# Top-k attention with an ELU feed-forward block: a prologue in written order on two queues, five smaller decoding buffers, and decoding moved to later steps

## The chip, the cores and the metric

The kernel runs on one core of a Trainium2 chip. The metric is the device time of one execution in microseconds (us). The engines are TensorE (PE, with its weight loads shown as PEld), VectorE (DVE), ScalarE (ACT), GpSimd (POOL) and SyncE (SP). SP here only issues DMAs.

## What is computed

Eight batches of eight heads, 576 rows, head size 64. For each row of scores only those at or above the 32nd largest enter the softmax. The result, put together to 4608 tokens of 512 values, goes through a feed-forward block with ELU between two matrix products. The weights `w_in` (512 x 2048) and `w_out` (2048 x 512) arrive as 64-bit floats.

```python
scores = scale * np.matmul(q, k.transpose(0, 1, 3, 2))
kth = np.partition(scores, -top_k, axis=-1)[..., -top_k:-top_k + 1]
scores = np.where(scores >= kth, scores, -1000000000.0)
attn = np.exp(scores - np.max(scores, axis=-1, keepdims=True))
attn = attn / (np.sum(attn, axis=-1, keepdims=True) + 1e-09)
x = np.matmul(attn, v)            # then (B,H,S,D) -> (B*S, H*D)
h = x @ w_in
g = np.where(h > 0.0, h, np.exp(np.minimum(h, 0.0)) - 1.0)
out = g @ w_out
```

## The kernel before

**Steps.** The attention work is cut into steps, each one tile of up to 128 query rows for two heads (a head pair). The scores of a step are 2 x 128 x 576. In step n the program makes the scores of step n + 2 (`scores`: eight PE products on L300, two ACT copies on L308), finds the 32 largest of each row of step n on DVE, and finishes steps n - 1 and n - 2: mask and exponential on ACT (`mask`, L369 and L370, after two small POOL operations, L366 and L368), division on POOL (`normalise`, L380 to L387), transposes (`turn`, L406 and L407), the product with v (`attend`, L432). Finding the 32 largest of a row takes four rounds of MAX8 with three MATCH_REPLACE8 between them (`select_row`: L319, L323, L329; `select`: L341, L346, L353).

**Two stages.** The first eight steps (`tight = 8`) cover two query tiles of batch 0: steps 0 to 3 are query tile 0 for the four head pairs, steps 4 to 7 query tile 1. They use `select_row`, and the order of instructions on each engine is left to a scheduler that works from priorities. From step 8 on `manual_schedule` keeps the order as written on PE, ACT, DVE and POOL.

**Feed-forward pieces.** When all heads of a block of tokens are through, `finish` (which copies the attention result to an `xT` tile) puts its feed-forward pieces on a list. `hidden` is one 128-wide slice of the hidden layer: PE products L490, three ACT operations (L502 to L504) that write `n` and `gT`, and later one DVE operation, the gate (L471), which closes it. `project` is a quarter of the second product (L513). `feed`, called four times a step, takes pieces from the list by their costs and due times, once the weights they need are marked as decoded. At most four `n` tiles are unclosed at once.

**Decoding.** The weights are 32 pieces of 128 x 512 64-bit floats. `load_weight` brings one into a `raw` tile by one DMA of 512 KB (L152). `convert_first` takes the exponent part to `e` and the low word to the mantissa part `m` by three ACT operations (L169, L170, L171) and a clamp on POOL (L172). `convert_last` shifts `e` (L179) and joins it with the high word (L182) on DVE, and POOL adds `e` and `m` into the weight tile (L186). `decode_piece(i)` loads piece i + 2, converts the first half of piece i and the last half of piece i - 1. `hook`, called from the selection, runs one `decode_piece`: after rounds 0 and 2 of each row, so four in a step. 33 calls end in step 8, where the memory of the raw tiles goes to the feed-forward pools `f`, `g` and `x`.

A raw tile is `4 * WN` words per partition, with three buffers: two parts for the 64-bit words, one for `e`, one for `m`.

```python
words = t[:, 0 : 2 * WN].rearrange("p (n w) -> p n w", w=2)
return words[:, :, 0], words[:, :, 1], t[:, 2 * WN : 3 * WN], t[:, 3 * WN :]
```

**Prologue.** All loads go to SP's queue in this order: k and q of head pair 0, weight pieces 0 and 1, k and q of pair 1, v of pair 0, then the rest. Each k or q of a head pair is three DMAs (128, 128 and 32 KB). `transpose_qk` turns k and q of a pair by PE (L258, L270) and copies them by ACT (L263, L276); then come the scores of step 0, and the same for pair 1 and step 1. This part too is left to the scheduler.

Of the kernel before, what the change touches and what calls it, by code (L numbers as in the profile page):

```python
# [8 lines left out]
AF = mybir.ActivationFunctionType  # L9
# [71 lines left out]
def kernel(  # L81
# [36 lines left out]
    small = pool("small", 4)  # L118
    xtpool = pool("xt", 2)
    opool = pool("o", 1)  # L120
# [7 lines left out]
    earlyf = raws.enter_context(tc.tile_pool(name="earlyf", bufs=4))  # L128
    rawpool = raws.enter_context(tc.tile_pool(name="raw", bufs=3))

# [19 lines left out]
    def load_weight(i):  # L150
        t = rawpool.tile([P, 4 * WN], U32, tag="raw", name="raw")
        nc.sync.dma_start(t[:, 0 : 2 * WN], weight(i)[0])  # L152
        raw[i] = t

    def parts(t):
        words = t[:, 0 : 2 * WN].rearrange("p (n w) -> p n w", w=2)
        return words[:, :, 0], words[:, :, 1], t[:, 2 * WN : 3 * WN], t[:, 3 * WN :]

    def convert_first(i):

        lo, hi, e, m = parts(raw[i])
# [4 lines left out]
        nc.gpsimd.tensor_scalar(  # L172
            ef, ef, (2.0 - 2.0**-3 - 2.0**-23) * 2.0**-32, 2.0**-63, ALU.min, ALU.max
        )

    def convert_last(i):
        t, dst = raw.pop(i), weight(i)[1]
        lo, hi, e, m = parts(t)
        nc.vector.tensor_scalar(  # L179
            e, e, 0x0FFFFFFF, 3, ALU.bitwise_and, ALU.logical_shift_left  # L180
        )
# [33 lines left out]
    def load_qk(b, hp):  # L215

        for name, src in (("k", k), ("q", q)):
            n = J + 1 if name == "k" else J
            t = ldpool.tile([P, n, 2, D], FP32, tag=name + "in", name=name + "in")
            if name == "k":  # L220
                last = t
            for hh in range(2):
                nc.sync.dma_start(
                    t[:, 0:J, hh, :],
                    src[b, 2 * hp + hh, 0:JP, :].rearrange("(p j) d -> p j d", j=J),
                )
            nc.sync.dma_start(
                last[0:R, J, :, :] if name == "k" else last[R:P, J, :, :],
                src[b, 2 * hp : 2 * hp + 2, JP:S, :].rearrange("h p d -> p h d"),
            )  # L230
            loaded[b, hp, name] = t
# [81 lines left out]
    def select_row(u, i):  # L313
# [8 lines left out]
        for r in range(TOP_K // 8 - 1):  # L322
# [130 lines left out]
    def finish(blk, parts, at, cols, src):  # L453
        if blk.xT is None:
            if blk.slots == 1 and late:
                blk.xT = late["x"].tile([P, NC, P], FP32, tag="xT", name="xT")
            else:
                blk.xT = xtpool.tile([P, NC, T], FP32, tag="xT", name="xT")
# [181 lines left out]
    for n in range(NS + 3):  # L640
# [22 lines left out]
        if n == tight:  # L663
            E = mybir.EngineType
            ctx.enter_context(
                tc.manual_schedule(engines={E.PE, E.Activation, E.DVE, E.Pool})
            )
        passes = select(cur) if cur else iter(range(4))
# [61 lines left out]
```

## Time and profile before

| | us |
|---|---|
| median of 3 runs | 1694.66 |
| range of the 3 runs | 1693.64 to 1695.99 |
| the profiled execution, its time | 1695.23 |
| the profiled execution, its span | 1693.4 |

Over the span PE is busy 1597.5 us (94%), DVE 1542.7 (91%), ACT 1179.6 (70%) and POOL 627.0 (37%). The span is the time from the first to the last instruction in the trace; the execution's own time has 1.83 us more around it. A group of instructions is given by its line in the program, its engine, its operation and the tiles it writes and reads. A row of a table by stretches gives, for each stretch of time, how long each engine was busy in it and with how many instructions (in brackets), then the clock that was granted to PE as a share of full speed, the busy share of the DMA engines and what they moved in GB/s. A line of the chain of waits names a piece of work that the end of the run depended on, with its start and its length.

Some rows that are used later, from the groups of the decoding lines (lowest, median and highest duration in ns over all 32 pieces):

| line | engine | operation | ns |
|---|---|---|---|
| L169 | ACT | absolute value of the high word | 647 / 673 / 706 |
| L170 | ACT | low word to float | 643 / 666 / 727 |
| L171 | ACT | float to integer | 612 / 620 / 661 |
| L172 | POOL | clamp | 612 / 612 / 1142 |
| L179 | DVE | mask and shift | 400 / 426 / 1487 |
| L182 | DVE | join with the high word | 667 / 677 / 1227 |
| L186 | POOL | add, to `w_in` | 1258 / 1270 / 1320 |

One operation begins before the one ahead of it on its engine has fully ended, so the distance from start to start on ACT and DVE is some 0.08 to 0.11 us shorter than the duration.

### The profile page before, as it was taken

Reading aid. Unit: us, or ns where it says so; the run is one execution under the profiler, and the core shown is the slowest. Engines: PE = TensorE matmul, PEld = TensorE weight load, DVE = VectorE, ACT = ScalarE, POOL = GpSimd, SP = SyncE. Lnnn points to the kernel's source line nnn. Section 1 sums busy time; section 2 is a strip of 40 time slices with the busy share of each in tenths; the row PEclk is TensorE's granted clock in tenths of the full one; section 3 lists DMA queues with packets and bytes.
Section 4 is the critical chain, followed back from the end, with each engine's and each line's share of the span. In section 5 each row is a group of like instructions: output and inputs, shape, how many; then the busy total and the mean of one; then the engine's idle time right before and its main releaser. Section 6 shows DMA issues by size and latency. Waiting matters only on the chain.

```text
span 1693.4 us, 26805 instructions
## 1 busy us (share of the span) xinstructions
PE 1597.5 (94%) x8560; PEld 1035.0 (61%) x8560; DVE 1542.7 (91%) x3248; ACT 1179.6 (70%) x2813; POOL 627.0 (37%) x1719
## 2 busy tenths in 40 slices
PE   4568899999999999999999999999999999999999
PEld 3355676667575666756557575755557575755565
DVE  6889999999999999999999999999998999998600
ACT  5787776778776776857758585867758686857531
POOL 3675333343333333433333333333333333332200
PEclk8568999999999999999999999999999999999999
DMA  5531021001200111001100111001100000000000
GB/s 156 169 130 63 15 56 36 7 1 42 51 12 7 29 35 42 1 14 42 43 19 1 28 42 35 7 10 46 36 20 8 21 21 28 7 7 7 7 13 13
DMA packets 101131, 56.25 MB, mean 33 GB/s; under 512 B 84096, under 2 KB 92288, under 8 KB 100992
## 3 DMA queue, kind: packets, MB, share of 16 engines
q1 hardware_dynamic: 100992, 54.55, 11.7%
q8 instruction: 68, 1.11, 0.3%
q14 instruction: 71, 0.58, 0.1%
HBM read 45.09 MB, written 9.44 MB: 32 GB/s over the span
## 4 chain that ended last, share of the span: by engine, by line
PE 68%; DVE 21%; ACT 5%; issue 2%; POOL 2%; DMA 1%; SPq 0%; ACTq 0%; POOLq 0%; DVEq 0%
PE ops L513 25%; PE hps L490 21%; PE avps L432 8%; DVE wk L346 7%; PE scps L300 7%; DVE m L353 6%; PE eps L406 5%; DVE m L341 2%; DVE gT L471 1%; DVE wk L323 1%; DVE m L329 1%; PE qkps L270 1%; ACT sc L370 1%; ACT sc L369 1%; ACT et L407 1%
## 5 line engine op out<-in xcount | busy, mean ns | idle before, releaser
L353 DVE MAX8 m<-wk 128x8 f32<-128x576 f32 x816 | 574.9, 745 | 0.0
L490 PE MATMUL hps<-xT,w_in 128*128 128x256 f32 (+2 forms) x2432 | 554.3, 376 | 19.3 <-ACT gT L503 19.3
L513 PE MATMUL ops<-w_out,gT 128*128 128x512 f32 x1152 | 522.6, 598 | 0.0
L490 PEld LDWEIGHTS hps<-xT,w_in 128*128 128x128 f32 x2432 | 409.5, 194 | 119.9 <-ACT gT L503 26.4
L346 DVE MATCH_REPLACE8 wk<-m,wk 128x576 f32<-128x576 f32 x544 | 399.4, 741 | 0.0
L513 PEld LDWEIGHTS ops<-w_out,gT 128*128 128x128 f32 x1152 | 208.4, 190 | 232.8 <-issue 201.0
L380 POOL TENSOR_SCALAR dene<-den 128x2 f32<-128x2 f32 x144 | 34.9, 243 | 819.6 <-ACT sc L370 819.0
L369 ACT ACTIVATE sc<-sc,neg 128x576 f32<-128x576 f32 x288 | 226.5, 787 | 56.6 <-POOL neg L366 56.1
L370 ACT ACTIVATE sc<-sc,gap 128x576 f32<-128x576 f32 x288 | 223.2, 775 | 26.6 <-ACT sc L369 1.9
L308 ACT ACTIVATE sc<-scps 128x576 f32<-128x576 f32 x288 | 173.4, 661 | 82.4 <-PE scps L300 82.4
L387 POOL TENSOR_SCALAR sc<-sc,rec 128x576 f32<-128x576 f32 x288 | 218.7, 769 | 15.2 <-POOL rec L385 0.4
L300 PE MATMUL scps<-kqT 64*128 64x288 f32 (+1 forms) x1280 | 198.1, 438 | 21.5 <-ACT sc L308 14.7
L471 DVE SCALAR_TENSOR_TENSOR gT<-n,gT 128x256 f32<-128x256 f32 (+2 forms) x304 | 129.1, 431 | 95.3 <-ACT n L504 95.3
L407 ACT COPY et<-eps 128x512 f32<-128x512 f32 x288 | 167.4, 581 | 61.8 <-PE eps L406 61.8
L406 PEld LDWEIGHTS eps<-ident,sc 128*128 128x128 f32 x1152 | 144.5, 145 | 93.4 <-issue 48.9
L346 DVE MATCH_REPLACE8 wk<-m,sc 128x576 f32<-128x576 f32 x272 | 199.7, 741 | 0.0
L432 PE MATMUL avps<-et,vT 128*64 128x256 f32 (+2 forms) x2080 | 191.0, 325 | 9.0 <-ACT et L407 8.4
L406 PE MATMUL eps<-ident,sc 128*128 128x128 f32 x1152 | 177.9, 280 | 21.8 <-POOL sc L387 18.6
L341 DVE MAX8 m<-sc 128x8 f32<-128x576 f32 x272 | 191.3, 744 | 0.0
L432 PEld LDWEIGHTS avps<-et,vT 128*64 128x64 f32 x2080 | 122.3, 140 | 80.4 <-issue 24.7
L502 ACT ACTIVATE n<-hps 128x256 f32<-128x256 f32 (+2 forms) x304 | 112.6, 370 | 84.2 <-PE hps L490 79.0
L300 PEld LDWEIGHTS scps<-kqT 64*128 64x128 f32 (+1 forms) x1280 | 106.0, 180 | 90.2 <-issue 45.1
(47 smaller groups left out, 1236.6 us busy)
## 6 DMA issues: line engine op xcount, KB each, us to landing
kin<-in_k_dram SPq DMA_DIRECT2D x64, 128.0 KB, 2.8
qin<-in_q_dram SPq DMA_DIRECT2D x64, 128.0 KB, 2.8
raw<-in_moe_w_in_dram SPq DMA_DIRECT2D x16, 512.0 KB, 3.9
vT<-in_v_dram SPq DMA_DIRECT2D x64, 128.0 KB, 2.3
raw<-in_moe_w_out_dram SPq DMA_DIRECT2D x16, 512.0 KB, 3.3
out_dram<-osb SPq DMA_DIRECT2D x32, 256.0 KB, 2.2
kin<-in_k_dram SPq DMA_DIRECT2D x32, 32.0 KB, 2.5
kin<-in_q_dram SPq DMA_DIRECT2D x32, 32.0 KB, 2.2
```

Of the source, the lines that this page charges most:

```text
L300: nc.tensor.matmul(wide[i][rows, half, 0:HS], kq[part, q0 : q0 + u.t.ql], kq[part, k0 : k0 + HS], start=True, stop=True,)
L341: nc.vector.max(found[i], cur[i])
L346: nc.vector.match_replace(wk[i], found[i], cur[i], TAKEN)
L353: nc.vector.max(found[i], cur[i])
L369: nc.scalar.activation(sc, sc, AF.Prelu, bias=neg[:], alpha=STEEP)
L370: nc.scalar.activation(sc, sc, AF.Exp, bias=gap[:], accum_out=u.den[:, i : i + 1])
L387: nc.gpsimd.tensor_scalar(u.sc[:, i, :], u.sc[:, i, :], rec[:, i : i + 1], 1.0, ALU.mult, ALU.mult)
L406: nc.tensor.transpose(ps[:, c * P : (c + 1) * P], sc[:, c0 : c0 + P], ident[:])
L407: nc.scalar.copy(g.et[:, chunks, u.at, :], ps[:, 0 : n * P].rearrange("p (c q) -> p c q", c=n),)
L432: nc.tensor.matmul(ps[i * D : (i + 1) * D, cols], vt[:, 2 * J + i if c == J else i * J + c, :], w, start=(c == 0), stop=(c == J),)
L490: nc.tensor.matmul(ps[:, 0:n_tok], w_in[:, i, f * P : (f + 1) * P], blk.xT[:, i, 0:n_tok], start=(i == 0), stop=(i == NC - 1),)
L513: nc.tensor.matmul(blk.o[:], blk.gT[f // NG][:, f % NG, s * P : (s + 1) * P], w_out[:, f, :], start=(f == 0), stop=(f == NF - 1),)
```

## The change

The prologue is written out inside `manual_schedule`, so PE, ACT, DVE and POOL keep its order. The q of head pair 0 is loaded through ACT's queue. Weight piece 0 is loaded after the k of pair 0, and piece 1 after k and q of pair 1.

A raw tile has three parts in place of four: the mantissa part is written over the low words, at their step of two words. There are five buffers in place of three (30 KB per partition in place of 24). The last half of a piece now follows its first half by two hooks in place of one, so there are 34 calls.

In `select_row` the hook moves: one per row (after round 2) while the query tile is 0, that is two in each of steps 0 to 3, and three per row after that, six in each of steps 4 to 7.

The `xT` tiles for blocks of one slot get a pool of three small buffers of their own from the start; the large `xT` tiles are placed in the memory that the raw tiles leave. The pool `f` of the `n` tiles for the later blocks has four buffers in place of five.

```diff
-    xtpool = pool("xt", 2)
+    xpool = pool("x", 3)
...
-    rawpool = raws.enter_context(tc.tile_pool(name="raw", bufs=3))
+    rawpool = raws.enter_context(tc.tile_pool(name="raw", bufs=5))
...
-        t = rawpool.tile([P, 4 * WN], U32, tag="raw", name="raw")
+        t = rawpool.tile([P, 3 * WN], U32, tag="raw", name="raw")
...
-        return words[:, :, 0], words[:, :, 1], t[:, 2 * WN : 3 * WN], t[:, 3 * WN :]
+        return words[:, :, 0], words[:, :, 1], t[:, 2 * WN :]
...
-        ef, mf = e.bitcast(FP32), m.bitcast(FP32)
+        ef, mf = e.bitcast(FP32), lo.bitcast(FP32)
...
-        nc.scalar.activation(m.bitcast(I32), mf, AF.Copy, bias=-(2.0**23))
+        nc.scalar.activation(lo.bitcast(I32), mf, AF.Copy, bias=-(2.0**23))
...
-            dst.bitcast(I32), e.bitcast(I32), m.bitcast(I32), ALU.add
+            dst.bitcast(I32), e.bitcast(I32), lo.bitcast(I32), ALU.add
...
-            late["f"] = ctx.enter_context(tc.tile_pool(name="f", bufs=5))
+            late["f"] = ctx.enter_context(tc.tile_pool(name="f", bufs=4))
...
-            late["x"] = ctx.enter_context(tc.tile_pool(name="x", bufs=2))
+            late["x"] = ctx.enter_context(tc.tile_pool(name="xt", bufs=2))
...
-        if i > 0:
-            convert_last(i - 1)
-            decoded[0] = i
+        if i > 1:
+            convert_last(i - 2)
+            decoded[0] = i - 1
...
-            n = J + 1 if name == "k" else J
+            n, queue = (J + 1, nc.sync) if name == "k" else (J, other)
...
+            if r == 2 or u.t.qt > 0:
+                hook()
             if r != 1:
-                hook()
                 yield
...
-    load_qk(0, 0)
-    for i in range(2):
-        load_weight(i)
+    E = mybir.EngineType
+    engines = {E.PE, E.Activation, E.DVE, E.Pool}
+    load_qk(0, 0, nc.scalar)
+    load_weight(0)
     load_qk(0, 1)
+    load_weight(1)
     load_v(0, 0)
-    start_qk(0, 0)
-    turn_qk(True)
-    scores(steps[0])
+    with tc.manual_schedule(engines=engines):
+        for hp in range(2):
+            start_qk(0, hp)
+            turn_qk(True)
+            scores(steps[hp])
     load_qk(0, 2)
-    start_qk(0, 1)
-    turn_qk(True)
-    scores(steps[1])
     load_qk(0, 3)
...
-    decode += [lambda i=i: decode_piece(i) for i in range(2 * NF + 1)]
+    decode += [lambda i=i: decode_piece(i) for i in range(2 * NF + 2)]
```

The lines of the changed kernel are one or two higher than those of before: L179 and L182 become L180 and L183, L186 becomes L187, L172 becomes L173, the selection's L319, L323 and L329 become L320, L324 and L330, the gate L471 becomes L473, and the ACT operations of `hidden` L504 to L506.

More of the change, by code (lines that the diff above doesn't have):

```diff
@@ L156, in parts @@
         words = t[:, 0 : 2 * WN].rearrange("p (n w) -> p n w", w=2)
-        return words[:, :, 0], words[:, :, 1], t[:, 2 * WN : 3 * WN], t[:, 3 * WN :]
+        return words[:, :, 0], words[:, :, 1], t[:, 2 * WN :]
     def convert_first(i):
-        lo, hi, e, m = parts(raw[i])
-        ef, mf = e.bitcast(FP32), m.bitcast(FP32)
+        lo, hi, e = parts(raw[i])
+        ef, mf = e.bitcast(FP32), lo.bitcast(FP32)
         nc.scalar.activation(ef, hi.bitcast(FP32), AF.Abs, scale=2.0**-48)
         nc.scalar.activation(mf, lo, AF.Copy, scale=2.0**-29, bias=2.0**23)
-        nc.scalar.activation(m.bitcast(I32), mf, AF.Copy, bias=-(2.0**23))
+        nc.scalar.activation(lo.bitcast(I32), mf, AF.Copy, bias=-(2.0**23))
         nc.gpsimd.tensor_scalar(
@@ L177, in convert_last @@
         t, dst = raw.pop(i), weight(i)[1]
-        lo, hi, e, m = parts(t)
+        lo, hi, e = parts(t)
         nc.vector.tensor_scalar(
@@ L208, in decode_piece, with load_qk @@
             convert_first(i)
-        if i > 0:
-            convert_last(i - 1)
-            decoded[0] = i
+        if i > 1:
+            convert_last(i - 2)
+            decoded[0] = i - 1
     loaded, kqT, vT = {}, {}, {}
-    def load_qk(b, hp):
+    def load_qk(b, hp, other=nc.sync):
         for name, src in (("k", k), ("q", q)):
-            n = J + 1 if name == "k" else J
+            n, queue = (J + 1, nc.sync) if name == "k" else (J, other)
             t = ldpool.tile([P, n, 2, D], FP32, tag=name + "in", name=name + "in")
@@ L222, in load_qk @@
             for hh in range(2):
-                nc.sync.dma_start(
+                queue.dma_start(
                     t[:, 0:J, hh, :],
@@ L226, in load_qk @@
                 )
-            nc.sync.dma_start(
+            queue.dma_start(
                 last[0:R, J, :, :] if name == "k" else last[R:P, J, :, :],
@@ L454, in finish @@
         if blk.xT is None:
-            if blk.slots == 1 and late:
-                blk.xT = late["x"].tile([P, NC, P], FP32, tag="xT", name="xT")
+            if blk.slots == 1:
+                blk.xT = xpool.tile([P, NC, P], FP32, tag="xT", name="xT")
             else:
-                blk.xT = xtpool.tile([P, NC, T], FP32, tag="xT", name="xT")
+                blk.xT = late["x"].tile([P, NC, T], FP32, tag="xT", name="xT")
         nc.scalar.copy(blk.xT[:, at, cols], src)
@@ L663 @@
         if n == tight:
[L664 to L667, printed above, removed]
+            ctx.enter_context(tc.manual_schedule(engines=engines))
         passes = select(cur) if cur else iter(range(4))
```

## The prediction

> **What bounds the kernel now.** I read the chain of waits first, then the busy times by stretch, cut at the first MAX8 (L319) of each of the eight row-wise steps, 0 to 7. The page's chain over the whole run says PE 68%, DVE 21%, but that is an average over stages. In order of time it begins so (start us, us, what):
>
> ```profile
> 6.52 5.87 DMA kin<-in_k_dram
> 12.52 0.45 PE qkps L270
> 12.97 2.27 PE scps L300 x8
> 15.24 0.64 ACT sc L308
> 15.91 1.41 DVE m L319 x2
> ...
> 56.76 6.62 DMA raw<-in_moe_w_in_dram x2
> ...
> 79.53 3.98 DMA raw<-in_moe_w_in_dram
> ```
>
> The first scores stood behind one transpose of the second head pair, which waited for its k until 12.52; later the chain runs through loads of raw weights. By step (stretch, length, busy us of PE, PEld, DVE, ACT, POOL; granted clock, DMA):
>
> ```profile
> 15.91:25.57 9.66, 6.36 (x43) 4.52 (x41) 9.66 (x21) 6.05 (x13) 1.96 (x5) 1.00 0.63 148
> 25.57:35.20 9.63, 3.89 (x15) 2.64 (x16) 9.63 (x21) 5.14 (x12) 4.04 (x13) 0.60 0.72 229
> 35.20:57.88 22.68, 11.29 (x53) 7.60 (x52) 18.71 (x34) 18.25 (x38) 15.34 (x23) 0.65 0.48 129
> 57.88:79.71 21.83, 11.64 (x43) 7.43 (x43) 18.63 (x32) 15.48 (x30) 15.33 (x24) 0.58 0.57 169
> 79.71:96.82 17.11, 9.49 (x39) 6.12 (x38) 14.32 (x27) 13.02 (x25) 12.50 (x20) 0.50 0.37 126
> 96.82:117.62 20.80, 17.03 (x79) 12.85 (x78) 18.81 (x37) 16.34 (x41) 15.02 (x22) 0.61 0.49 151
> 117.62:134.57 16.95, 13.48 (x98) 11.07 (x98) 16.40 (x35) 15.35 (x42) 10.77 (x19) 0.90 0.36 125
> 134.57:150.28 15.71, 10.06 (x55) 8.75 (x55) 14.84 (x30) 13.14 (x36) 11.78 (x19) 0.78 0.32 101
> ```
>
> A step of selection alone is 9.65 us of DVE without a gap. From 35.20 to 150.28 DVE is idle for 3.97 + 3.20 + 2.79 + 1.99 + 0.55 + 0.87 = 13.4 us. The waits name nearly all of it (who <- for whom: us in all, times, longest):
>
> ```profile
> DVE raw L179 <- POOL raw L172: 25.2, 12, 11.2
> ```
>
> Take off the 11.2 before the first piece and the 1.2 before the second: 12.7 is decoding. From 160 to 254 the chain is almost all DVE, which is 100% busy there; after that PE carries most of it. So up to about 254 us **DVE sets the time, and PE has slack**. In the built programs PE's order is the same from step 9 on, and the FFN pieces fall on the same calls of `feed`, all 304 hidden pieces of them. What DVE gains before step 8 should therefore shift the whole rest, PE's part too.
>
> **The prologue.** Six loads on SP take 4.05 us to issue (0.72 to 4.77), and the last lands at 6.77. With q on ACT's queue both halves are issued by about 2.8. The Trainium skill (DMA: Bandwidth & Descriptors, "Issuing engines are not separate DMA queues") speaks against more: the queues share the same 16 DMA engines and only issue time is saved. The row: 5 to 10 us moved 243 GB/s with the engines 88% busy. The 576 KB of the first pair need 2.4 us at that rate, so they land near 5; only the 2.0 us of issue are won (by counting a second queue as bandwidth it would be over 3). But ACT now has all three conversions of weight 0 (1.65 us at their pitches of 0.57, 0.57, 0.53) ahead of the first key copies. Weight 0 is issued near 3 and lands near 7 (1,088 KB at 243 GB/s after a start at 2.4); copies 8.8 to 10.1, scores to 12.4. Then ACT has two conversions of weight 1 ahead of the score copies, and that weight moved behind the second k and q, issued near 7.5: at 3.9 to landing (its row on the page) 11.8, with bytes alone 11.4. Conversions to 12.95, first score copy 13.6; DVE's first MAX8 stands behind weight 1 on DVE too (clamp 13.0, its two operations to 14.1). So first MAX8 between 14.1 and 15.7; I take 14.5, **1.4 us** early. The issues on ACT stand ahead of its table load, 1.28 us, due only at 7: no cost.
>
> **The decoding.** Per piece ACT does three operations, POOL two (0.61 and 1.27), DVE two. DVE's price: busy 124.0 us from 15.91 to 153.25 (step 8's second MAX8), less 77.9 for selection and 8.0 for 15 gate operations, over 29 pieces, is 1.31. The floor is 0.94 (0.43 + 0.68 less overlaps of 0.17); in steps 2 and 3, about 11.5 pieces, it is (18.71 + 18.63 - 19.3) / 11.5 = 1.57.
>
> The Trainium skill (SBUF — State Buffer, "Who interferes with whom") has DVE and POOL lock a port pair for a whole instruction, the later one blocked until the other ends. Row: L179 runs 0.40 to 1.49 us, so blocking for most of POOL's 1.27 is seen. By the rule, if every piece met an add in full, a piece would be 0.94 + 1.27 = 2.2 and the 24 pieces of steps 4 to 7 would cost 53 us; by the row at six a step, 38. In the new order a piece's last DVE operation is followed after one selection operation (0.67) by the next piece's first, so an add started at once hits it for some 0.6: near 1.5. I take 1.5, ends 1.31 and 1.57.
>
> Not in the trace: POOL's add with one operand at an 8-byte step (lo in place of the removed packed m). Below: no change, 1.27, as nothing gets shorter; above: half more, 1.9, which the skill (GPSIMD Engine Reference, "Performance pitfalls for Q7 kernels") gives only for steps over 8 bytes. This is exactly 8, so I take 1.27. ACT's last conversion likewise goes from 0.62 towards the strided L170, 0.67: 0.3 us a step, hidden.
>
> DVE's account, from 14.5: steps 0 and 1, 19.3; steps 2 and 3, 19.3 + 4 pieces x 1.31 = 24.5 and 0.5 of gaps: step 4 begins at 58.8, where it was 79.71. Steps 4 to 7: 38.6 + 24 x 1.5 = 36.0 + about 14 gate operations, 7.5, gives 82.1. Beside it ACT needs 24 x 1.65 + 4 x 5.2 (scores, masks, transposes' copies) + 16 x 0.52 = 69, and POOL 24 x 1.88 + 4 x 4.3 = 62: neither is the bound, but both are over 75% full. **Gaps:** in steps 2 and 3 of before, 3.6 a step, where three buffers make load wait for the last add of an earlier piece. Five buffers hold a piece over all five hooks from its load to its add, so the load goes three hooks (about 10 us) before use against 3.9 to land, and the add comes two hooks after the conversion. So not 3.6 but what steps 6 and 7 show, 0.7: 2.8. Step 8 at 58.8 + 82.1 + 2.8 = 143.7, plus one more piece left for step 8, 1.0: 144.7 against 153.3, **8.6 us earlier**.
>
> **Behind step 8.** The FFN's n buffers go from five to four: ACT's L502 then waits for the gate (L471) of four pieces back. By the times in the trace this would bite some eight times between 180 and 236, by 0.1 to 2.8 us. Queued behind it on ACT are masks and score copies, needed by DVE over 10 us later, and PE's next hidden piece; PE is idle 4.1 us between 230 and 260, which takes that up. Cost 0, at worst 1. Single-slot xT tiles get three buffers of their own, which releases nothing that is late. If PE's slack were gone, each such wait would count in full, some 10 us.
>
> Sum: 8.6 less about 0.3, some 8.3. The profiled execution took 1695.23 (span 1693.4): it would be 1686.9. The runs' median is 1694.66, 0.57 lower: **1686.3**.
>
> **Rivals.**
> 1. *The relay stalls* (slower). Six pieces a step over ACT, POOL and DVE, each in order: a mask's wait on POOL holds the clamp, the clamp DVE. If the gap in steps 4 to 7 stays 3.6 a step, 14.4 in place of 2.8, the gain is -3.3: 1698. It decides from 2.8 a step on. For: ACT 83% and POOL 75% full there, and before's waits on POOL's clamp. Against: those had raw loads in their chain, and gaps shrank to 0.55 and 0.87 where loads came in time. The same end comes from a strided add of 1.9 (24 x 0.63 = 15 us).
> 2. *PE takes it back* (no change). PE carries the later chain; if its work before step 8 could not move up, the end stays: 1694.5. Against: in steps 4 to 7 PE needs about 50 us of 85, at a clock of 0.50 to 0.90.
> 3. *Nothing is in the way.* Pieces at 1.31 and no gaps: 4.6 + 2.8 more: 1679.
> 4. The prologue does nothing (weight 1 lands late, first MAX8 at 15.9): 1.4 less, 1687.7; inside the forecast.
>
> **How the numbers follow.** Forecast with its neighbours (1682 to 1691): 0.63. Rival 1: 0.14, half of it beyond +0.2%. Rival 2: 0.08. Rival 3: 0.15. The measurement tells 0.2%, 3.4 us, from no change. Below 1691.3: the forecast nearly whole and rival 3, 0.78; within 3.4 us: 0.11; slower, rival 1's longer gaps or a dearer add: 0.11. Range 1679.5 to 1694.5: rival 3 at its low end, rival 2 at its high end.
>
> **What shows it.** Right: first MAX8 at 14 to 15.7; step 4 near 59; L180 waiting for POOL's clamp under 5 us in all after the first piece; step 8 near 144; the chain from 160 to 254, moved up, still DVE. Wrong: gaps over 2 us a step before L180; POOL's add over 1.5 us; L180 and L183 together over 1.8 a piece; or step 8 early and the end not.

## The result, and the profile after

| | before | after |
|---|---|---|
| median of 9 runs, us | 1694.48 | 1690.41 |
| range, us | 1691.62 to 1696.05 | 1689.52 to 1691.92 |
| ratio, 95% interval | | 0.9976 [0.9966, 0.9987] |
| the profiled execution, its time | 1695.23 | 1689.76 |
| the profiled execution, its span | 1693.4 | 1687.8 |

The kernel is 0.24% faster: 4.07 us between the medians, 2.2 to 5.8 by the interval, where 8.3 were forecast. In a second set of runs the two kernels stood at 0.998 [0.9972, 0.9989].

The same steps as stretches, cut at the first MAX8 of each step; the eight rows of before stand in the prediction. Columns: stretch, length, busy time with instructions of PE, PEld, DVE, ACT and POOL, granted clock, DMA share, GB/s.

```profile
15.43:25.08 9.65, 7.63 (x44) 4.96 (x42) 9.65 (x21) 6.20 (x13) 2.27 (x7) 1.00 0.52 126
25.08:34.72 9.64, 6.09 (x20) 3.74 (x21) 9.64 (x21) 6.90 (x15) 4.37 (x12) 0.64 0.79 257
34.72:46.29 11.57, 11.57 (x44) 7.50 (x43) 11.57 (x26) 9.70 (x21) 6.86 (x15) 0.50 0.70 192
46.29:57.80 11.51, 11.51 (x44) 8.08 (x45) 11.51 (x25) 9.64 (x21) 7.72 (x14) 0.50 0.41 126
57.80:77.97 20.17, 12.99 (x49) 8.37 (x49) 20.17 (x34) 16.00 (x32) 15.46 (x24) 0.58 0.36 115
77.97:99.06 21.09, 13.51 (x63) 10.61 (x61) 20.78 (x36) 16.91 (x42) 16.73 (x24) 0.58 0.51 164
99.06:123.33 24.27, 17.73 (x113) 14.37 (x111) 21.36 (x39) 20.67 (x52) 19.53 (x28) 0.78 0.44 138
123.33:146.59 23.26, 15.19 (x78) 10.83 (x79) 21.51 (x39) 18.55 (x49) 15.86 (x22) 0.78 0.31 106
```

Steps 2 and 3 shrank from 44.5 us to 23.1: two pieces each, DVE never idle. The decoding that left them came back in steps 4 to 7, which grew from 70.6 to 88.8; DVE is idle there for 0.31 + 2.91 + 1.75 us (length less busy time, row by row). The waits of DVE from 30 us on (who <- for whom: us in all, times, longest) put all of it in front of three shifts, 4.9 us:

```profile
DVE raw L180 <- POOL raw L173: 4.9, 3, 2.9
```

Step 9 begins at 159.18, where it began at 164.43 before. What lies behind it takes 1528.6 us, and took 1529.0. So the 5.3 us won by step 9 are nearly the whole gain of the span (5.6), and nothing is seen to be lost behind. From 154 to 248 us DVE is still full:

```profile
154.00:248.00 94.00, 81.61 (x645) 61.20 (x644) 93.97 (x209) 67.71 (x195) 35.64 (x101) 0.96 0.13 32
```

The chain that ended last tells less here than the prediction wanted of it: between 154 and 248 it now names PE and ACT beside DVE (L348, MATCH_REPLACE8, 17.8%; L515, a PE product, 14.8%), though DVE has 0.03 us of idle time in this stretch. DVE's operations are 41% of the chain there, and were 98% of it from 160 to 254 us before. I read this as two paths of nearly equal length, of which the view shows one; that is not shown further.

### The profile page after: what moved, and what is told of

Same layout as the page of the kernel before. It is cut to its first block, busy times and chain, and to the rows that moved or that the text cites. A ratio compares the mean times of both kernels' runs of the same rounds, so it can differ in the third digit from the quotient of the medians.

```text
span 1687.8 us, 26813 instructions
## 1 busy us (share of the span) xinstructions
PE 1603.6 (95%) x8560; PEld 1038.0 (61%) x8560; DVE 1547.1 (92%) x3248; ACT 1179.9 (70%) x2813; POOL 634.7 (38%) x1719
## 4 chain that ended last, share of the span: by engine, by line
PE 62%; DVE 23%; ACT 4%; issue 1%; POOL 0%; ACTq 0%; DVEq 0%
PE ops L515 23%; PE hps L492 20%; DVE wk L348 10%; DVE m L355 8%; PE avps L434 7%; PE scps L301 6%; PE eps L408 5%; DVE m L343 3%; DVE gT L473 2%; PE qkps L271 1%; ACT sc L371 1%; ACT et L409 1%; ACT sc L372 1%; PE scps L408 1%; ACT n L506 1%
## 5 line engine op out<-in xcount | busy, mean ns | idle before, releaser
L515 PE MATMUL ops<-w_out,gT 128*128 128x512 f32 x1152 | 523.4, 599 | 0.0
L348 DVE MATCH_REPLACE8 wk<-m,wk 128x576 f32<-128x576 f32 x544 | 398.8, 739 | 0.0
L515 PEld LDWEIGHTS ops<-w_out,gT 128*128 128x128 f32 x1152 | 208.8, 190 | 233.4 <-issue 200.7
L309 ACT ACTIVATE sc<-scps 128x576 f32<-128x576 f32 x288 | 173.4, 661 | 75.1 <-PE scps L301 74.9
L473 DVE SCALAR_TENSOR_TENSOR gT<-n,gT 128x256 f32<-128x256 f32 (+2 forms) x304 | 128.5, 430 | 92.5 <-ACT n L506 92.5
L348 DVE MATCH_REPLACE8 wk<-m,sc 128x576 f32<-128x576 f32 x272 | 199.4, 739 | 0.0
L504 ACT ACTIVATE n<-hps 128x256 f32<-128x256 f32 (+2 forms) x304 | 112.5, 370 | 81.1 <-PE hps L492 74.7
```

Of the source, the lines that this page charges most:

```text
L348: nc.vector.match_replace(wk[i], found[i], cur[i], TAKEN)
L515: nc.tensor.matmul(blk.o[:], blk.gT[f // NG][:, f % NG, s * P : (s + 1) * P], w_out[:, f, :], start=(f == 0), stop=(f == NF - 1),)
```

## The experiments

In what follows "the price" of a piece is DVE's busy time in a group of steps less 9.65 us a step for selection and less its gate operations (each from its start to that of the next instruction on DVE), divided by the pieces. "Gaps" is DVE's idle time, in waits of over 0.15 us. Ratios are to the kernel before, run beside on the same chip: its median was between 1691.1 and 1694.6 us from one set of runs to the next, so times of different sets are not compared.

### What each part is worth

The changed kernel with one part taken back: the hook as before, four pieces a step (e5); the old prologue (e6); three raw tiles in place of five (e7).

```diff
-            if r == 2 or u.t.qt > 0:
-                hook()
             if r != 1:
+                hook()
                 yield
```

> The changed kernel with the hook where it was (after rounds 0 and 2 of each row, four pieces a step in all eight steps). Theory (a piece costs DVE more the closer together the pieces are, since the adds on POOL then meet them): from step 2 on four to five pieces a step at 1.2 to 1.35 each, steps 4 to 7 at 70 to 76 us in place of 88.8, steps 2 and 3 at 29 to 34 in place of 23.1; step 9 at 153 to 158, so as good as the changed kernel or up to 6 us better. Rival (few pieces in the first steps is what helps, since ACT and POOL are then free for attention): steps 2 and 3 go back to over 38 us and step 9 to 162 or later.

```diff
-    load_qk(0, 0, nc.scalar)
-    load_weight(0)
+    load_qk(0, 0)
+    for i in range(2):
+        load_weight(i)
     load_qk(0, 1)
-    load_weight(1)
...
-    with tc.manual_schedule(engines=engines):
-        for hp in range(2):
...
```

> The changed kernel with the prologue of before: one queue, weights 0 and 1 ahead of k and q of pair 1, the scheduler's order. Theory (the prologue won 0.5 us): first MAX8 at 15.7 to 16.2, step 9 at 159.5 to 160, the whole within 1 us of the changed kernel. Rival (the prologue carries most of the gain of 4): the whole some 3 us longer than the changed kernel.

```diff
-    rawpool = raws.enter_context(tc.tile_pool(name="raw", bufs=5))
+    rawpool = raws.enter_context(tc.tile_pool(name="raw", bufs=3))
```

> The changed kernel with three raw buffers of three parts in place of five, two hooks between the halves of a piece as in the change. A load of piece i + 2 then waits for the add of piece i - 1, which comes one hook before piece i + 2 is converted: about 3.3 us for 3.9 of loading. Theory (before's idle time in steps 2 to 5 came from too few buffers): gaps in steps 4 to 7 rise from 4.9 to 15 us or more, step 9 to 168 or later, and the whole is slower than the kernel before. Rival (buffers were not the limit, but the number of pieces in a step): step 9 stays within 3 us of 159.2.

And the kernel before with one part put in: the hook of the change (g1), its prologue (g2), its tiles and pools (g3); beside the changed kernel once more (f1). The edits are the hunks of the change.

> The kernel before, with only the hook moved (two pieces a step, then six): old prologue, three four-part raw tiles, one hook between the halves of a piece. Theory, the three parts work only together: with three tiles the load of a piece waits for the add of the piece three before, so the gaps in steps 4 to 7 are 12 us or more and the time is within 0.2% of before or slower. Rival, moving the hook is the change and the rest is small: steps 4 to 7 have gaps of 5 to 7 us, the time 0.15 to 0.3% less.

> The kernel before, with only the new prologue. Theory: first MAX8 0.3 to 0.5 us early and step 2 less than 1 us early, where steps 2 to 7 still wait for loads: the time within 0.1% of before. Rival, the prologue is worth 0.3% by itself, as taking it back from the changed kernel cost: 5 us less.

> The kernel before, with only the buffers changed (five tiles of three parts, two hooks between the halves, the pools of x and four n tiles): hook and prologue as before. Theory: the gaps in steps 2 and 3 fall from 7.1 to 5 or 6 us (the first loads come late whatever the buffers), those of steps 4 to 7 from 6.2 to 4 or less, and the time is 0 to 0.15% less. Rival, the buffers are what matters: all gaps under 3 us in sum, 0.3% or more less.

> The changed kernel once more, on the same chip as the next three, so that their traces and times have a neighbour. Theory: 0.2 to 0.3% below the kernel before, first MAX8 at 15.4 to 15.7, step 9 at 158 to 160, gaps in steps 4 to 7 of 4 to 6 us. Rival (the gaps and prices in the first trace are chance from one execution to another): step 9 differs from 159.18 by more than 2 us.

| kernel | hook | prologue | tiles | ratio, interval | first MAX8 | step 4 | step 9 | gaps, steps 2, 3 / 4 to 7 |
|---|---|---|---|---|---|---|---|---|
| before | | | | 1 | 15.91 | 79.71 | 164.43 | 7.1 / 6.2 |
| g2 | | new | | 1.0007 [0.9998, 1.0016] | 15.54 | 79.17 | 165.24 | 5.8 / 8.9 |
| g3 | | | new | 1.0000 [0.9992, 1.0009] | 15.92 | 80.44 | 163.38 | 7.0 / 4.0 |
| g1 | new | | | 1.0033 [1.0021, 1.0046] | 16.05 | 62.89 | 170.76 | 4.4 / 15.9 |
| e5 | | new | new | 0.9999 [0.9989, 1.0008] | 15.58 | 78.43 | 161.76 | 5.6 / 4.3 |
| e7 | new | new | three small | 1.0003 [0.9993, 1.0012] | 15.66 | 58.10 | 162.55 | 0 / 11.4 |
| e6 | new | | new | 1.0008 [0.9998, 1.0017] | 15.65 | 60.49 | 162.83 | 2.0 / 5.7 |
| after | new | new | new | 0.9976 [0.9966, 0.9987] | 15.43 | 57.80 | 159.18 | 0 / 4.9 |
| f1 | new | new | new | 0.9980 [0.9972, 0.9989] | 15.64 | 58.31 | 158.88 | 0 / 5.4 |

No part gives anything alone, and any two of them are within 0.1% of before. Four expectations failed: g3's gaps in steps 2 and 3 (5 to 6 us, measured 7.0), e5's step 9 (153 to 158, measured 161.76), e6's time (within 1 us of the changed kernel, measured some 5 us longer), and e7's step 9 and gaps (168 or later and 15 us, measured 162.55 and 11.4). In the table, step 9 of e5, e6 and e7 comes 1.6 to 2.7 us before that of the kernel before, which their ratios do not show. In their set of runs before took 1691.1 us, 3.4 less than in the first set; no trace of before was taken beside them, so this stays unexplained.

The hook alone makes the kernel slower, and 15.9 us of gaps arise in steps 4 to 7, as g1's theory had it (12 or more). The theory's cause, loads that wait for an add three pieces back, the trace does not show: ACT stands for raw loads for 2.7 us in all from 30 to 150 us. In front of the longest gap (6.1 us, up to 84.53) the conversion comes late because ACT keeps its order: copies of transposes stand ahead of it, for which PE waited 5.44 us until POOL's two multiplications were through. That is a stall of the kind of rival 1 of the prediction, and of its size.

What the tiles do to the loads is seen in the other runs. From 30 to 150 us ACT stands for raw loads for 8.9 us in the kernel before, not at all in g3, 2.7 us in the changed kernel and 13.9 in e7. But without these waits g3 has the gaps of before in steps 2 and 3, 7.0 us. Its longest (g3's timeline, ACT, POOL and DVE):

```profile
50.23 0.68 ACT L170 ACTIVATE raw<-raw 128x512 f32<-128x512 f32 x1
...
54.92 0.23 POOL L381 TENSOR_SCALAR dene<-den 128x2 f32<-128x2 f32 x1
...
56.89 1.48 POOL L388 TENSOR_SCALAR sc<-sc,rec 128x576 f32<-128x576 f32 x2
58.45 1.20 POOL L173 TENSOR_SCALAR raw<-raw 128x512 f32<-128x512 f32 x2
59.10 0.83 DVE L180 TENSOR_SCALAR raw<-raw 128x512 uint32<-128x512 uint32 x1 [2.70 <-POOL raw L173]
```

The piece's conversion (L170) is done at 50.91. Its clamp (L173) stands behind two adds and the division of a step (L381 to L388), and DVE behind the clamp.

f1 repeats the trace of after: gaps of 0.87, 2.91 and 1.65 us in the same places. They are not chance.

The old prologue (e6) cost 0.32% in the ratios, though it moved the first MAX8 by only 0.2 us. Its trace differs by 3.65 at step 9: 0.2 at the start, 2.5 in steps 2 and 3, 1.0 in steps 4 to 7. The 2.5 are mostly one wait; e6's timeline (start, length, engine, what, in brackets the idle time before it):

```profile
35.81 0.59 ACT L409 COPY et<-eps 128x512 f32<-128x512 f32 x1
36.28 0.68 ACT L170 ACTIVATE raw<-raw 128x512 f32<-128x512 f32 x1
37.06 0.62 POOL L173 TENSOR_SCALAR raw<-raw 128x512 f32<-128x512 f32 x1 [2.21 <-ACT raw L170]
37.71 0.43 DVE L180 TENSOR_SCALAR raw<-raw 128x512 uint32<-128x512 uint32 x1 [2.02 <-POOL raw L173]
```

and the changed kernel's, where the same conversion comes 5 us sooner and stands for its load only:

```profile
31.32 0.67 ACT L170 ACTIVATE raw<-raw 128x512 f32<-128x512 f32 x1 [2.74 <-DMA raw<-in_moe_w_in_dram]
32.08 0.61 POOL L173 TENSOR_SCALAR raw<-raw 128x512 f32<-128x512 f32 x1 [0.65 <-ACT raw L170]
```

In e6 the scheduler had placed ACT's copies of transposes ahead of that conversion. The written prologue is worth little at the start; it is worth something because the order that the scheduler makes after it is another one.

### Behind step 8

Five `n` tiles in place of four.

```diff
-            late["f"] = ctx.enter_context(tc.tile_pool(name="f", bufs=4))
+            late["f"] = ctx.enter_context(tc.tile_pool(name="f", bufs=5))
```

> The changed kernel with five n buffers again in the pool f; nothing else. Theory (the shortfall arises before step 8, in the crowded steps 4 to 7, and what DVE gains by step 9 is carried to the end): no difference, within 0.5 us of the changed kernel, some 4 to 5.5 us under the kernel before; first MAX8 of step 9 at 159.2. Rival (part of the gain is given back behind step 8, by ACT waiting for the gate of four pieces back): the end comes 2 to 4 us earlier, with step 9 still at 159.2.

1689.68 us, ratio 0.9978 [0.9969, 0.9987], against 0.9976 of the changed kernel; 1529.4 us from step 9 to the end of the span, against 1528.6. Going down to four buffers costs nothing that can be seen. In all eighteen traces of this study the rest behind step 9 takes 1526.3 to 1529.9 us, wherever step 9 begins, from 151.94 (e2) to 201.57 (e8). So what is won or lost by step 9 goes through to the end, and the missing half of the forecast is not behind step 8. The two traces of the changed kernel differ by 2.2 us in this rest (1528.6 and 1526.4), so nothing smaller can be told from it.

### The gaps: POOL

The scaling of the probabilities in the first eight steps left out (e2), or done by ACT (f2).

```diff
+        if u.early:
+            return
         for i in range(2):
             nc.gpsimd.tensor_scalar(
...
+                    prev.early = True
                     normalise(prev)
```

> The changed kernel without the two POOL multiplications of scores by the reciprocal (L389) in the first eight steps: the softmax of these steps is not divided by its sum. Frees POOL of 1.48 us a step, in the stretch in which the clamp of a weight piece waits behind them. Theory (the gaps of 4.9 us before L180 in steps 4 to 7 come from POOL's order, with the clamp behind the normalisation and an add): gaps fall to under 2 us, step 9 some 3 to 4 us earlier, near 155.5, and the whole some 3 to 4 us shorter. Rival (ACT's load in steps 4 to 7 holds the pieces back): gaps stay at 4 to 5 us, step 9 within 1 us of 159.2.

```diff
         for i in range(2):
+            if u.early:
+                nc.scalar.activation(
+                    u.sc[:, i, :], u.sc[:, i, :], AF.Copy, scale=rec[:, i : i + 1]
+                )
+                continue
             nc.gpsimd.tensor_scalar(
...
```

> The changed kernel, with the scaling of the probabilities of the first eight steps (L389) done by ACT in place of POOL; the computation is whole. Theory, POOL's order makes the gaps in front of the shift (L180): with two 1.5 us operations a step taken off POOL the gaps in steps 4 to 7 fall from 4.9 to under 1 us, the price of a piece stays at 1.5 to 1.6, step 9 is at 152 to 156 and the time 3 to 7 us less than that of the changed kernel. Rival, the gaps are ACT's (its conversions come late, and it is over 75% full): 1.3 us more a step on ACT makes the gaps as long or longer, 5 to 10 us, and step 9 is not before 159.

| kernel | ratio, interval | price, step 4 to step 9 | gaps, step 4 to step 9 | step 9 |
|---|---|---|---|---|
| after | 0.9976 [0.9966, 0.9987] | 1.55 | 4.9 | 159.18 |
| f1 | 0.9980 [0.9972, 0.9989] | 1.51 | 5.4 | 158.88 |
| e2 | 0.9929 [0.9913, 0.9946] | 1.47 | 0.0 | 151.94 |
| f2 | 0.9942 [0.9929, 0.9954] | 1.35 | 5.9 | 153.44 |

Here the price is taken from step 4 to step 9, over 26 pieces, since the scheduler moved some of them into step 8 in f2. In e2 the two multiplications, 1.48 us of POOL a step, are gone, and so is every gap. Step 9 comes 7.2 us earlier, twice what was expected: 4.9 us are the gaps, and 2.6 us are DVE's busy time, which fell too. The largest gap of the changed kernel shows how they make it (its timeline, lines of PE and others left out):

```profile
103.87 0.23 POOL L382 TENSOR_SCALAR dene<-den 128x2 f32<-128x2 f32 x1
...
105.37 0.68 ACT L170 ACTIVATE raw<-raw 128x512 f32<-128x512 f32 x1
...
106.42 1.48 POOL L389 TENSOR_SCALAR sc<-sc,rec 128x576 f32<-128x576 f32 x2
...
107.86 1.30 POOL L187 TENSOR_TENSOR w_out<-raw 128x512 int32<-128x512 int32 x1
...
109.25 0.61 POOL L173 TENSOR_SCALAR raw<-raw 128x512 f32<-128x512 f32 x1
...
109.83 1.30 POOL L187 TENSOR_TENSOR w_out<-raw 128x512 int32<-128x512 int32 x1
109.89 1.51 DVE L180 TENSOR_SCALAR raw<-raw 128x512 uint32<-128x512 uint32 x1 [2.91 <-POOL raw L173]
```

ACT's conversion (L170) is done at 106.05. The clamp that needs it starts at 109.25, since POOL, which keeps its order, first ends the division (from 103.87, 4 us with the two multiplications) and an add. DVE stands for 2.91 us. ACT is not what it waits for. In the other two gaps, too, the clamp begins 2.2 and 4.4 us after its conversion, directly behind a multiplication. The last two lines show the price as well: the shift starts 0.06 us after an add and takes 1.51 us in place of 0.43.

f2 hit its time and its step 9, but not in the way that its theory said. Before 128 us its gaps are small, then three of 0.68, 1.88 and 1.84 us come back at the last pieces, which the scheduler had packed closer:

```profile
DVE raw L180 <- POOL raw L173: 1.5, 3, 0.7
```

```profile
DVE raw L180 <- POOL raw L173: 4.4, 3, 1.9
```

(the wait rows of f2, from 20 to 128 us and from 128 to 160). The gain is in the price: by the durations of L180 and L183 its 26 pieces take 38.1 us of DVE, against 42.6 in f1, and its gate operations 5.8 against 7.3. So less work on POOL pays in either of two ways, as shorter waits or as fewer meetings with DVE, and which of the two it is depends on the order. f2 computes everything, and no kernel of this study that does is faster (f4, further down, is equal to it within its interval): 1682.94 us, 0.38% below the changed kernel on the same chip (0.9942 / 0.998).

g4 was to tell order from load, with the five short operations of the reciprocal moved ahead in the program.

```diff
...
+                    if prev:
+                        reciprocal(prev)
                 elif prev:
-                    normalise(prev)
+                    prev.normal = True
+                    scaling(prev)
```

> The changed kernel, with the division in the first eight steps in two places: the five short POOL operations of the reciprocal (L382 to L387) at the first row's selection, the two multiplications (L389) where they were; POOL's work is the same. Theory, the gaps come from the order on POOL, a clamp (L173) behind a block of 4 us: with the block cut to 1.5 us the gaps in steps 4 to 7 fall to 2.5 us or less, step 9 at 155 to 157.5, the time 1.5 to 4 us less than that of the changed kernel. Rival, the gaps come from the sum of POOL's work: 4 to 6 us of gaps as before, only elsewhere, step 9 at 158 to 160.

0.998 [0.9971, 0.9989], gaps of 0.30, 2.90 and 1.63 us. It told nothing: the scheduler put the reciprocal back beside the scaling in steps 6 and 7, and POOL's order there is that of the changed kernel. Whether another order of the same work would close the gaps stays open. That POOL's load alone does not make them is shown by the next run.

### The price of a piece

POOL's add replaced by a fill of the weight tile (e3).

```diff
-        nc.gpsimd.tensor_tensor(
-            dst.bitcast(I32), e.bitcast(I32), lo.bitcast(I32), ALU.add
-        )
+        nc.gpsimd.memset(dst, 0.01)
```

> The changed kernel with the POOL add of a weight piece (L187) replaced by a POOL memset of the same weight tile: the decoded weights are left out, and the feed-forward result with them. POOL then reads nothing from SBUF in that place and is busy for a shorter time. Theory (a piece costs DVE 1.55 us in steps 4 to 7 because POOL's adds meet L180 and L183 there, against 0.95 where there are two in a step): the pieces cost 1.0 to 1.15, steps 4 to 7 take 10 to 14 us less than 88.8, step 9 comes at 145 to 149, and the whole is 10 to 13 us shorter than the changed kernel. Rival (the price is the order of DVE's own instructions, or ACT is the limit): steps 4 to 7 stay within 4 us of 88.8.

1684.91 us, ratio 0.9947 [0.9932, 0.9962], so some 5 us under the changed kernel and not the 10 to 13 expected; step 9 came at 154.45 and not at 145 to 149. A fill waits for nothing, so the scheduler moved all of them into the first 26 us, and steps 4 to 7 have neither add nor fill. These four steps take 75.4 us in place of 88.8, as expected. The price there is 1.03, where it was 1.60 and, in f1, 1.56. So meeting the add costs DVE 0.5 to 0.6 us a piece. The 14 gate operations in these steps fell as well, from 6.9 to 3.5 us.

The gaps grew to 8.5 us, though POOL is busy for only 35.7 of the 75.4 us, 47%. In four of the five gaps, 8.3 us, the clamp begins 1.9 to 2.2 us after its conversion, and POOL has gone on with the division in between. So it is the block ahead of the clamp that makes the gaps, and no high busy share of POOL is needed for it. ACT, busy for 72.6 of the 75.4 us, has a part in when the block comes: the division waits for its exponentials four times in these steps, 8.1 us in all.

The start shows DVE meeting POOL's fills alone, and where step 9 lost its time (e3's timeline, POOL and DVE):

```profile
14.94 2.85 POOL L187 MEMSET w_in<- 128x512 f32 x6
15.03 8.18 DVE L180 TENSOR_SCALAR raw<-raw 128x512 uint32<-128x512 uint32 x1 [2.97 <-POOL raw L173]
17.74 5.19 POOL L187 MEMSET w_out<- 128x512 f32 x11
22.98 0.51 POOL L243 MEMSET vT<- 64x64 f32 x2
23.13 1.40 DVE L318 MAX8 m<-sc 128x8 f32<-128x576 f32 x2
```

One shift of 0.43 us took 8.18, while sixteen further fills of 0.52 us followed one another on POOL without a pause, and the first MAX8 came 7.7 us late behind it. No theory had that in its expectation.

Is the price set by how close pieces follow one another? Four pieces in each step, with loads early enough (f3), and the same with ACT's scaling (f4):

```diff
-            if i + 2 < 2 * NF:
+            if 3 <= i < 2 * NF - 2:
...
-            if r == 2 or u.t.qt > 0:
-                hook()
             if r != 1:
+                hook()
...
+    for i in range(2, 5):
+        load_weight(i)
```

> Four pieces in each of the first eight steps, with the new prologue and five buffers, and weight pieces 2 to 4 loaded ahead of v of pairs 1 to 3, so that the first pieces do not wait for their loads. Theory, the price of a piece depends on how close pieces follow one another (0.9 to 1.1 at two or four a step, 1.5 to 1.6 at six): 32 pieces at 1.1 in eight steps save some 8 us of DVE time, gaps stay under 5, step 9 at 153 to 157. Rival, the price is set by what POOL does beside it in the early steps, not by spacing: the pieces of steps 1 to 3 cost 1.5 as in the kernel with four a step run before (1.52 in steps 2 and 3), and step 9 is at 159 to 162.

> The two edits above together. Theory: gaps under 1 us a pair of steps and the lower price, step 9 at 149 to 154, 5 to 10 us less than the changed kernel. Rival, ACT becomes the bound where conversions of four pieces and the scaling meet: gaps return, step 9 not before that of the better of the two alone.

f3: 0.9985 [0.9976, 0.9994], step 9 at 160.45; its pieces cost 1.17 in steps 0 and 1, 1.65 in steps 2 and 3, 1.53 in steps 4 to 7. The theory falls: four a step can be nearly as dear as six. f4: 0.9946 [0.9934, 0.9959], step 9 at 155.81, no better than f2 alone. The count of pieces in a step does not set the price: at four a step in steps 4 to 7 it is 1.53 in f3, 1.31 in e5 and 1.13 in f4. That work on POOL beside a piece makes it dear is shown for the add alone (e3): without the multiplications the pieces of steps 2 and 3 cost 1.64 in f4, as much as in f3.

### The start

Both weights after k and q of pairs 0 and 1 (e4).

```diff
     load_qk(0, 0, nc.scalar)
-    load_weight(0)
     load_qk(0, 1)
+    load_weight(0)
     load_weight(1)
```

> The changed kernel with weight pieces 0 and 1 loaded behind k and q of head pairs 0 and 1. Theory (the prologue won 0.5 us and not 1.4 because ACT converts weight 0 ahead of the first key copies and weight 1 ahead of the score copies, each after its landing at 8.4 and 12.9): the key copies no longer wait, the first scores end some 1.8 us earlier on PE, near 12, but the first MAX8 stays behind both weights on DVE and behind one conversion of each on ACT, so it comes between 14.0 and 15.5, 0 to 1.4 us earlier. Rival (the landing of k and q, at 6.2, sets the start): PE's first scores stay at 11.6 and the first MAX8 at 15.4.

1703.33 us, 1.0055 [1.004, 1.007]. ACT's timeline in e4:

```profile
6.96 0.32 ACT L264 COPY kqT<-scps 128x192 f32<-128x192 f32 x1 [2.92 <-PE scps L259]
...
12.59 0.66 ACT L170 ACTIVATE raw<-raw 128x512 f32<-128x512 f32 x1 [3.33 <-DMA raw<-in_moe_w_in_dram]
...
15.08 1.17 ACT L309 ACTIVATE sc<-scps 128x576 f32<-128x576 f32 x2
```

and in the changed kernel:

```profile
8.42 0.66 ACT L170 ACTIVATE raw<-raw 128x512 f32<-128x512 f32 x1 [4.37 <-DMA raw<-in_moe_w_in_dram]
...
10.24 0.30 ACT L264 COPY kqT<-scps 128x192 f32<-128x192 f32 x1
...
12.88 0.67 ACT L170 ACTIVATE raw<-raw 128x512 f32<-128x512 f32 x1 [1.37 <-DMA raw<-in_moe_w_in_dram]
13.45 0.65 ACT L171 ACTIVATE raw<-raw 128x512 f32<-128x512 uint32 x1
14.00 1.18 ACT L309 ACTIVATE sc<-scps 128x576 f32<-128x576 f32 x2
```

In e4 the keys were copied 3.3 us sooner, but ACT then stood 3.33 us for the first weight, whose conversions stand ahead of the score copies, and the first MAX8 came at 17.89. In both kernels the score copy (L309) ends a chain of weight conversions and not of keys. The early first MAX8 that e4's theory expected did not come. Steps 4 and 5 then got 12.4 us of gaps, and the time went the same way.

### The written order up to the end

`manual_schedule` from the prologue on, so that the first eight steps keep the program's order too (e8).

```diff
-    with tc.manual_schedule(engines=engines):
-        for hp in range(2):
...
+    ctx.enter_context(tc.manual_schedule(engines=engines))
+    for hp in range(2):
...
```

> The changed kernel with the written order kept from the prologue to the end, so that in the eight first steps too the scheduler moves nothing. ACT then has both steps' score copies ahead of the weights, and a clamp or a normalisation stands where the program puts it. Theory (the scheduler's places cost the start 2 to 3 us and the gaps 4.9): first MAX8 at 12 to 13, 2.5 to 3.4 earlier. In the eight steps I expect a second effect of unknown size, as each row's MAX8 and MATCH_REPLACE8 now follow each other directly: if such dependent pairs cost no more than others, step 9 comes at 148 to 154; if each of the 14 a step costs 0.1 to 0.2 more, at 160 or later. Rival (the start is set by the loads): first MAX8 at 15 or later.

1731.89 us, 1.0236 [1.0221, 1.0251]. The first MAX8 came at 12.94, the earliest of all, but the first step of selection took 11.2 us in place of 9.65, steps 4 to 7 had 25 us of gaps, and step 9 came at 201.57. DVE's timeline in e8:

```profile
14.59 0.76 DVE L330 MAX8 m<-wk 128x8 f32<-128x576 f32 x1
15.38 0.09 DVE L324 MATCH_VALUE_LOAD wk<-m,wk 128x8 f32 x1
15.46 0.74 DVE L324 MATCH_REPLACE8 wk<-m,wk 128x576 f32<-128x576 f32 x1
16.23 0.76 DVE L330 MAX8 m<-wk 128x8 f32<-128x576 f32 x1
```

From one MAX8 to the next, with the MATCH_REPLACE8 between them, it is 1.64 us here. In the changed kernel the scheduler had interleaved the two rows of a step, so that each operation stands behind one that it does not need, and the same two take 0.67 and 0.72:

```profile
15.43 1.41 DVE L320 MAX8 m<-sc 128x8 f32<-128x576 f32 x2
16.77 0.07 DVE L324 MATCH_VALUE_LOAD wk<-m,sc 128x8 f32 x1
...
17.48 0.08 DVE L324 MATCH_VALUE_LOAD wk<-m,sc 128x8 f32 x1
...
18.21 1.41 DVE L330 MAX8 m<-wk 128x8 f32<-128x576 f32 x2
```

(15.43 to 16.77 for two MAX8, 16.77 to 18.21 for two MATCH_REPLACE8). The 0.25 us on six such pairs are 1.5 of the 1.6 us.

## Why the forecast was half right

**Right.** DVE sets the time up to step 8, and what it wins there shifts everything behind, PE too. The waits of ACT for raw loads fell, from 8.9 to 2.7 us between 30 and 150 us. POOL's add with an operand at a step of 8 bytes takes 1.29 us (median; 1.27 before), so that step costs next to nothing, and ACT's last conversion went from 0.62 to 0.68. Four `n` buffers cost nothing that can be seen (e1). Of the signs, first MAX8 (15.43), step 4 (57.80), L180's waits after the first piece (4.9 us, with 5 as the bound) and the pair L180 and L183 (0.72 + 0.84 a piece over all 32, 0.83 + 0.90 in steps 4 to 7) were inside. Step 8 near 144 was not: 146.59. Nor was the chain from 154 to 248 still DVE by the view, and step 6 alone has 2.9 us of gaps (1.2 a step on average, with 2 as the bound).

**Wrong in the gaps and in size.** The sum's terms, as predicted and as traced, in us at step 9:

| term | predicted | traced | difference to the gain |
|---|---|---|---|
| first MAX8 | 14.5 | 15.43 | -0.9 |
| steps 0 to 3 | 44.3 | 42.4 | +1.9 |
| gaps, steps 4 to 7 | 2.8 | 4.86 | -2.1 |
| DVE busy, steps 4 to 7 | 82.1 | 83.9 | -1.8 |
| before's step 8, as the mark | 153.3 | 152.6 | -0.7 |
| the extra piece in step 8 (by difference) | 1.0 | 0.7 | +0.3 |
| sum | 8.6 | 5.3 | -3.3 |

- *"in steps 2 and 3 of before, 3.6 a step, where three buffers make load wait for the last add of an earlier piece"*, and with it *"So not 3.6 but what steps 6 and 7 show, 0.7: 2.8"*, is the step that failed. It gave the gaps to the loads, and took them to go with five buffers. g3 has five buffers and no wait of ACT for a load, and 7.0 us of gaps in steps 2 and 3. What makes most of them (4.7 of the 7.0) is the order on POOL: a clamp stands behind the division of a step, as in the changed kernel's largest gap, where the conversion was done 3.2 us before. The trace of before had it already. In seven of its ten gaps from step 2 on, 9.1 of 12.7 us, the clamp begins 2.3 to 4.0 us after its conversion, with multiplications of the division in between. One of them (before, ACT, POOL and DVE):

```profile
87.05 0.66 ACT L169 ACTIVATE raw<-raw 128x512 f32<-128x512 f32 x1
...
88.85 1.48 POOL L387 TENSOR_SCALAR sc<-sc,rec 128x576 f32<-128x576 f32 x2
90.29 1.27 POOL L186 TENSOR_TENSOR w_in<-raw 128x512 int32<-128x512 int32 x1
91.65 0.61 POOL L172 TENSOR_SCALAR raw<-raw 128x512 f32<-128x512 f32 x1
...
92.30 0.43 DVE L179 TENSOR_SCALAR raw<-raw 128x512 uint32<-128x512 uint32 x1 [2.04 <-POOL raw L172]
```

  Rival 1 had this mechanism, and what was held against it, raw loads in the chain, does not hold. With the two multiplications off POOL (e2) the 4.9 us are gone. POOL's share of the time, 75% in the prediction and 67.6 of 88.8 us in the trace, was right, and tells nothing here: at 47% (e3) the gaps are longer.
- *"near 1.5. I take 1.5"*: 1.60 and 1.56 in the two traces of the changed kernel. e3 shows that 0.5 to 0.6 of it is the meeting with the add, as the prediction's row (0.40 to 1.49 us for one shift) suggested. The working was right and the value low: 24 x 0.10 = 2.4 us more, of which cheaper gate operations (6.9 in place of 7.5) gave 0.6 back. The 8.0 us that the prediction read for 15 gate operations of before were those of 14.
- *"so they land near 5; only the 2.0 us of issue are won"* and *"I take 14.5"*: k and q of the first pair were issued by 3.01 and landed at 6.03, where they had landed at 6.64, so 0.6 us were won. The 243 GB/s were those of 5 to 10 us; from 2 to 5 us the changed kernel moved 200. Weight 0 landed at 8.40 in place of 7, and weight 1 at 12.86 in place of 11.8. ACT's order, which the prediction told, then did what it said. e4 shows that it is these conversions, not the keys, that set the time.
- *"144.7 against 153.3"*: in before the two first MAX8 of step 8 lie apart (150.28 and 153.25), in after side by side, from 146.59. The mark that answers to 146.59 is 153.25 less one pitch of 0.67, 152.6; the pitch was counted as gain.
- The prologue as *"**1.4 us** early"*, and rival 4, *"The prologue does nothing"*, both took the prologue as a matter of its own start. By e6 it is worth 0.3%, most of it in the trace through the order in steps 2 and 3; by g2 it is worth nothing alone. Such a part has no price of its own, which the sum assumed throughout.

Steps 0 to 3 were cheaper than predicted (0.94 a piece, the floor, and no gap) and gave 1.9 back. That was luck: nothing in the working led to it. Without it the gain at step 9 would have been some 3.4.

The span gained 5.6 us and the medians 4.07. Most of the difference is which executions were profiled: that of before took 0.75 us more than its median, and that of after 0.65 less than its own.

## What to carry to other kernels

Where a piece of work goes over three engines that each keep their order, price its spacing by the longest block of other work that can stand ahead of it, not by the busy shares: here DVE waited behind POOL at 76% busy and at 47%. Before a gap is given to its cause, look when the operation that ended it could have begun, and what its engine did until then. Take edits that depend on one another (more pieces a step, more buffers, an earlier start) as one, since each of these three alone brought nothing or a loss. And when DVE is the bound, look at what POOL does beside it: moving 1.5 us a step from POOL to ACT was worth 0.38%, more than the whole change.

## What was not expected of the hardware

- A DVE operation of 0.43 us was stretched to 8.18 us beside a row of fills on POOL without a pause (e3). The Trainium skill (SBUF — State Buffer, "Who interferes with whom") has whichever of DVE and POOL issues first hold the ports that they share for its whole instruction, with the other blocked; here sixteen POOL instructions began and ended, by the profile, before DVE's one was through.
- A MAX8 and MATCH_REPLACE8 that each need the result of the one just ahead take 1.64 us from start to start, interleaved with another row's 1.39 (e8 and after).
